# The first sixteen rows of wq, from column 4608 on, sent as transfers of their own from SyncE and GpSimd

## The chip, the cores and the metric

The kernel runs on one core of one Trainium2 chip. The metric is the device time of one execution in microseconds (us); three executions of the kernel before gave 675.35, 675.76 and 675.85, a median of 675.76.

## The reference, cut to what matters

One decode step for two sequences: an attention over a cache of 4096 positions with 16 heads of 256, and a small feed-forward, mixed by a gate. All numbers are float32.

```
g = sigmoid((x * gate_w).sum(-1))                    # x: 2 x 1 x 448
q = x @ wq                                           # wq: 448 x 4096, 16 heads of 256
p = softmax(q . k_cache / 16)                        # 2 x 16 heads x 4096 positions
a = (p . v_cache) @ wo                               # wo: 4096 x 448
b = relu(x @ w1) @ w2                                # 448 x 1792 x 448
out = g * a + (1 - g) * b
```

The two caches hold 32 units (sequence and head), each with 4 MB of keys and 4 MB of values. Every byte of them is used once.

## The kernel before, in words

All operands are laid out on the host so that a load is a plain block: 128 rows, one for each partition, and a contiguous run in each row. `kv` holds the 32 units, each 128 rows of 16,384 numbers (8,192 KB); `wq` is 128 rows of 14,336; `w12` (w1 and w2) 128 rows of 12,544; `wo` 128 rows of 14,336; `xg` (x and gate_w) 128 rows of 12. Three SBUF buffers, `slot0` to `slot2`, take the large loads in turn (L110, L116).

SyncE (SP) issues every large load, in the order in which they are to run (L121 to L144): wq into slot2, the first two units into slot0 and slot1, then in a loop (L126) one unit for each buffer that VectorE has released, and in `late` (L135) w12 in two parts and wo in five, cut at the columns of `CUTS` (L98). ScalarE issues xg (L121). Before each load into a used buffer SP takes the semaphore `free` of that buffer (L63 to L65), which VectorE's last multiplication on that buffer raises (L269). So SP has always asked for one whole unit beyond the one that is under way.

TensorE first waits for xg, computes the gate, then waits for wq and computes q (L187 to L224). From there each unit goes through three engines: TensorE multiplies query and keys (L242), ScalarE takes the exponential (L254), VectorE takes the maximum (L261) and multiplies by the values (L265). Behind the loop TensorE does the feed-forward from w12, and the projection with wo in steps `k` (L364): each of the five parts of wo has a semaphore of its own, and TensorE waits for it at the step where that part begins. The last part holds one step of 32. The result is copied once (L389) and stored (L394).

GpSimd (POOL) only makes an identity matrix (L148, L149), which VectorE reads at L155.

Of the kernel before, what the change touches and what calls it, by code (L numbers as in the profile page):

```python
# [6 lines left out]
AX = mybir.AxisListType  # L7

P, HP = 128, 64
G = 4  # L10
R = P // G
SLOTS = 3
NB = 2
ENGINES = ("tensor", "vector", "scalar", "gpsimd", "sync")
# [48 lines left out]
def take(e, sem, n=1):  # L63
    e.wait_ge(sem, n)
    e.sem_inc(sem, -n)  # L65


def gated_mix_decode(nc, xg, kv, wq, w12, wo, out):
    U, _, LEN = kv.shape
    KC, B = xg.shape[1], xg.shape[2] - 1  # L70
    KF = KC - 1
    D = KF * P + HP
    H = U // B
# [3 lines left out]
    S = LEN // (2 * T)  # L77
    SG = S // G
    NF = w12.shape[1] // 2 // D
    DG = D // G  # L80
    FG = NF * P // G
    RB = R // B
    HB = H // NB
    UB = U // NB
    HH = HB // G
    CW = 512
# [4 lines left out]
    def sbuf(name, *shape):  # L91
        return nc.alloc_sbuf_tensor(name, [*shape], F32).ap()

    def bank(name, n=CW):
# [2 lines left out]
    NO = NB * HH * J  # L97
    CUTS = (0, NO - 18, NO - 8, NO - 4, NO - 1, NO)  # L98
    TAIL = 8
    names = [*ENGINES, "xg", "w2", *(f"wo{k}" for k in CUTS[1:]), "query", "score", "top", "prob", "room",  # L100
             *(f"land{s}" for s in range(SLOTS)), *(f"free{s}" for s in range(SLOTS)), "out"]
    sem = {n: nc.alloc_semaphore(n) for n in names}
    land = [sem[f"land{s}"] for s in range(SLOTS)]
    free = [sem[f"free{s}"] for s in range(SLOTS)]
    pr = Program(nc)
    pe, dve, act, pool, sp = ENGINES
# [3 lines left out]
    slot = [sbuf(f"slot{s}", P, LEN) for s in range(SLOTS)]  # L110
# [5 lines left out]
    def load(s, src, signal, lo=0, hi=None):  # L116
        hi = src.shape[1] if hi is None else hi
        return lambda e: e.dma_start(slot[s][:, lo:hi], src[:, lo:hi]).then_inc(signal, 16)  # L118

    xg_sb = sbuf("xg_sb", P, KC, B + 1)  # L120
    pr.raw(act, lambda e: e.dma_start(xg_sb, xg).then_inc(sem["xg"], 16))  # L121
    pr.raw(sp, load(2, wq, land[2]))
    for u in range(2):
        pr.raw(sp, load(u, kv[u], land[u]))

# [9 lines left out]
    def late(e):  # L135
# [4 lines left out]
        for lo, hi in zip(CUTS, CUTS[1:]):  # L140
            load(0, wo, sem[f"wo{hi}"], lo * D, hi * D)(e)
        take(e, free[1])

    pr.raw(sp, late)  # L144

    ident = sbuf("ident", P, P)

# [1 line left out]
    have_ident = pr.op(pool, lambda e: e.affine_select(  # L149
        out=ident, in_=ident, compare_op=ALU.not_equal, fill=1.0, base=0, pattern=[[-1, P]], channel_multiplier=1),  # L150
        have_ident)


    sel = sbuf("sel", P, R)
    t = pr.op(dve, lambda e: e.tensor_reduce(sel, ident.rearrange("p (g r) -> p r g", g=G), axis=AX.X, op=ALU.add),  # L155
              have_ident)
    fsum = sbuf("fsum", P, B)
    t = pr.op(dve, lambda e: e.tensor_reduce(fsum, sel.rearrange("p (b r) -> p b r", b=B), axis=AX.X, op=ALU.add), t)
# [3 lines left out]


    xr = sbuf("xr", P, KC, G, B, RB)
    pr.raw(dve, lambda e: e.wait_ge(sem["xg"], 16))
    for g in range(G):
        pr.op(dve, lambda e, g=g: e.tensor_copy(xr[:, :, g], xg_sb[:, :, :B, None].to_broadcast([P, KC, B, RB])))  # L167
    xu = sbuf("xu", P, KC, UB // B, B)
# [5 lines left out]
    def flat(a):  # L174
        return a.rearrange("p b r -> p (b r)")

    def mm(out, lhs, rhs, start, stop, *after):
        return pr.op(pe, lambda e: e.matmul(out, lhs, rhs, start=start, stop=stop), *after)  # L178
# [4 lines left out]
    def activate(out, src, fn, *after, **kw):  # L183
        return pr.op(act, lambda e: e.activation(out, src, fn, **kw), *after)  # L184


    pr.raw(pe, lambda e: e.wait_ge(sem["xg"], 16))  # L187
    for c in range(KC):
        r = rows_of(c)
        t = mm(pw[0][:, :1], xr[r, c].rearrange("p g b r -> p (g b r)"), xg_sb[r, c, B:], c == 0, c == KC - 1, have_x)  # L190
# [4 lines left out]
    for c in range(KC):  # L195
        r = rows_of(c)
        t = mm(pw[1][:UB, :1], xu[r, c].rearrange("p u b -> p (u b)"), xg_sb[r, c, B:], c == 0, c == KC - 1)
# [3 lines left out]

    qt = sbuf("qt", P, T, U)
    W = 2 * KF * DH
    WQ = wq.shape[1] // NB
    wide = sbuf("wide", P, CW)
    pr.raw(pe, lambda e: take(e, land[2], 16))
    busy = [(), ()]
    for i in range(NB):
        w = slot[2][:, i * WQ:(i + 1) * WQ]
        for c in range(KC):  # L210
            for g in range(G):
                r = rows_of(c, g // 2)
                at = g * W + c * CW if c < KF else G * W + g % 2 * CW
                lhs, rhs = flat(xr[r, c, g]), w[r, at:at + CW]
                last = mm(pw[2 + i][g * R:(g + 1) * R, :], lhs, rhs, c == 0, c == KC - 1)
        t = activate(wide, pw[2 + i], AF.Copy, last, *busy[1], scale=SCALE)
# [4 lines left out]
        for s in range(2):  # L221
            dst = qt.rearrange("p t (i g s b) -> p i s t g b", i=NB, g=G, s=2)[:, i, s]
            src = pt[:, ::RB].rearrange("p (s t g b) -> p s t g b", s=2, t=T, g=G)[:, s]
# [7 lines left out]
    prob = sbuf("prob", P, SG)  # L231
    query = [sbuf(f"query{s}", P, T) for s in range(SLOTS)]
# [94 lines left out]
    w1, w2 = slot[2][:, :NF * D], slot[2][:, NF * D:]  # L327
    pr.raw(pe, lambda e: take(e, land[2], 16))
    half = NF * D // 2
    for c in range(KC):  # L330
        for g in range(G):
            j, i = divmod(g, 2)
            at = i * half + (j * KF + c if c < KF else 2 * KF) * FG
            r = rows_of(c, j)
            t = mm(ph[g * R:(g + 1) * R, :FG], flat(xr[r, c, g]), w1[r, at:at + FG], c == 0, c == KC - 1)
    t = activate(hs, ph[:, :FG], AF.Relu, t, have_omg, *busy[1], scale=omg)
# [23 lines left out]
    n = NO - TAIL  # L360
# [3 lines left out]
    def project(lo, hi):  # L364
        for k in range(lo, hi):
            if k in CUTS:
                pr.raw(pe, lambda e, s=sem[f"wo{CUTS[CUTS.index(k) + 1]}"]: e.wait_ge(s, 16))
            if k < n:
                g = k % G
                t = mm(acc[g * R:(g + 1) * R, :], lhs(k), w[:, k * D:(k + 1) * D], False, k >= n - G,  # L370
                       have_ot[k // (HH * J)])
            else:
                for g in range(G):
                    t = mm(z[g * R:(g + 1) * R, :DG], lhs(k), w[:, k * D + g * DG:k * D + (g + 1) * DG], k == n,
                           k == NO - 1)
        return t

    at = 0
# [3 lines left out]
    t = project(at, n)  # L382
    t = pr.op(dve, lambda e: e.tensor_copy(a_sb, acc), t)  # L383
# [3 lines left out]
    t = project(CUTS[-3], NO)  # L387
    res = sbuf("res", P, DG)
    t = pr.op(dve, lambda e: e.tensor_copy(res, z[:, :DG]), t)  # L389
# [66 lines left out]
```

## Time and profile before

| what | us |
|---|---|
| three executions, median (range) | 675.76 (675.35 to 675.85) |
| the profiled execution | 675.61 |
| its span, first to last instruction | 674.3 |
| outside the span | 1.3 |
| DMA queue of SP, share of 16 engines' span | 99.3% |
| bytes moved | 289.66 MB |
| VectorE busy | 341.5 |
| TensorE busy | 215.7 |
| ScalarE busy | 59.8 |
| first load (wq), issue to landing | 19.6 |

An engine of the core and a DMA engine are different things. The core has five engines that compute or issue (PE, VectorE as DVE, ScalarE as ACT, GpSimd as POOL, SyncE as SP); the 16 DMA engines move the bytes of the transfers that SP, ACT and POOL issue. A group of instructions is named by its line, its engine and its operation, then what it writes and reads; in brackets stands the idle time before it and what ended that. The DMA share of a window is the mean busy share of the 16 DMA engines in it; a packet is booked whole where it starts, so that short windows with long packets can show more than 1.

### The profile page before, as it was taken

Reading aid. Unit: us, or ns where it says so; the run is one execution under the profiler, and the core shown is the slowest. Engines: PE = TensorE matmul, PEld = TensorE weight load, DVE = VectorE, ACT = ScalarE, POOL = GpSimd, SP = SyncE. Lnnn points to the kernel's source line nnn. Section 1 sums busy time; section 2 is a strip of 40 time slices with the busy share of each in tenths; the row PEclk is TensorE's granted clock in tenths of the full one; section 3 lists DMA queues with packets and bytes.
Section 4 is the critical chain, followed back from the end, with each engine's and each line's share of the span. In section 5 each row is a group of like instructions: output and inputs, shape, how many; then the busy total and the mean of one; then the engine's idle time right before and its main releaser. Section 6 shows DMA issues by size and latency. Waiting matters only on the chain. (4 is left out here: it accounts for less than half of the span.)

```text
span 674.3 us, 4158 instructions
## 1 busy us (share of the span) xinstructions
PE 215.7 (32%) x1323; PEld 65.4 (10%) x1323; DVE 341.5 (51%) x571; ACT 59.8 (9%) x121; POOL 0.7 (0%) x6
## 2 busy tenths in 40 slices
PE   0633221333332123333321233333222333331376
PEld 0210000001001000100100010010000001000022
DVE  0015566544556664454656545455665544556662
ACT  0020001001000100100010010000001001000010
POOL 0000000000000000000000000000000000000000
PEclk9975567767655676776567677665567667656789
DMA  9999999999999999999999999999999999999997
GB/s 381 428 435 436 436 435 435 435 435 435 435 435 435 435 435 435 435 432 435 435 435 435 435 435 435 435 435 435 432 435 435 435 435 435 435 435 435 393 439 309
DMA packets 6052, 289.66 MB, mean 430 GB/s; under 512 B 928, under 2 KB 1056, under 8 KB 1312
## 3 DMA queue, kind: packets, MB, share of 16 engines
q1 hardware_dynamic: 5904, 289.60, 99.3%
q8 instruction: 3, 0.05, 0.0%
q10 hardware_dynamic: 144, 0.01, 0.0%
q14 instruction: 1, 0.01, 0.0%
HBM read 289.54 MB, written 0.06 MB: 429 GB/s over the span
## 5 line engine op out<-in xcount | busy, mean ns | idle before, releaser
L265 DVE SCALAR_TENSOR_TENSOR slot<-slot,prob 128x1024 f32<-128x1024 f32 x256 | 295.9, 1220 | 65.3 <-DVEq L65 65.3
L242 PE MATMUL ps<-slot,query 128*32 128x512 f32 x1024 | 184.0, 880 | 410.8 <-PEq L65 410.7
L261 DVE TENSOR_REDUCE nm<-ps 128x1024 f32 (+1 forms) x32 | 39.2, 1224 | 229.7 <-DVEq L65 229.7
L242 PEld LDWEIGHTS ps<-slot,query 128*32 128x32 f32 x1024 | 53.2, 154 | 539.9 <-issue 539.8
L254 ACT ACTIVATE prob<-ps,nm 128x1024 f32<-128x1024 f32 x32 | 35.7, 1114 | 384.6 <-ACTq L65 384.5
L254 ACT ACT_TABLE_LOAD x10 | 12.8, 1283 | 163.3 <-ACTq L65 163.3
L265 DVE DVE_READ_ACCUMULATOR slot<-slot,prob (+1 forms) x256 | 21.0, 82 | 0.0
L178 PE MATMUL pw<-slot,xr 128*32 128x512 f32 (+3 forms) x96 | 12.4, 646 | 1.4 <-PEq L65 1.4
L167 DVE COPY xr<-xg_sb 128x128 f32<-128x128 f32 x4 | 0.6, 221 | 18.2 <-DMA xg_sb<-in_xg 18.2
L178 PE MATMUL pw<-xg_sb,xr 128*128 128x1 f32 (+1 forms) x8 | 1.9, 352 | 21.4 <-DVE xu L169 21.4
L178 PE MATMUL acc<-slot,ot 128*32 128x448 f32 x48 | 5.9, 545 | 4.1 <-DMA slot<-in_wo 4.1
L249 ACT ACTIVATE query<-qt 128x2 f32 (+1 forms) x32 | 6.2, 193 | 0.0
L254 ACT ACTIVATION_READ_ACCUMULATOR prob<-ps,nm (+1 forms) x32 | 6.2, 193 | 0.0
L178 PE MATMUL acc<-slot,hr 128*32 128x448 f32 x28 | 4.9, 808 | 2.2 <-DMA slot<-in_w 2.2
L181 PE MATMUL pw<-ident,nm 128*16 128x128 f32 x2 | 0.7, 330 | 12.6 <-DVEq L315 12.6
L178 PEld LDWEIGHTS pw<-xg_sb,xr 128*128 128x128 f32 (+1 forms) x8 | 1.8, 320 | 21.4 <-DMA xg_sb<-in_xg 21.4
L178 PEld LDWEIGHTS pw<-slot,xr 128*32 128x32 f32 (+1 forms) x96 | 2.9, 119 | 9.4 <-issue 9.4
L383 DVE COPY wide<-acc 128x448 f32<-128x448 f32 x1 | 0.6, 625 | 4.9 <-PE pw L178 4.9
L181 PE MATMUL pw<-ident,wide 128*128 128x128 f32 x11 | 1.9, 288 | 2.4 <-ACT wide L184 2.4
L309 DVE COPY ot<-pw 128x256 f32<-128x256 f32 x4 | 1.5, 420 | 1.4 <-PE pw L178 1.4
L178 PE MATMUL pw<-slot,ot 128*32 128x112 f32 x64 | 2.2, 261 | 0.0
L301 DVE TENSOR_TENSOR os<-ov,pw 128x128 f32<-128x128 f32 x2 | 0.6, 288 | 3.0 <-PE pw L178 3.0
(42 smaller groups left out, 20.6 us busy)
## 6 DMA issues: line engine op xcount, KB each, us to landing
slot<-in_wq SPq DMA_DIRECT2D x1, 7168.0 KB, 19.6
slot<-in_w SPq DMA_DIRECT2D x2, 3136.0 KB, 30.5
slot<-in_wo SPq DMA_DIRECT2D x1, 3136.0 KB, 20.7
slot<-in_wo SPq DMA_DIRECT2D x1, 2240.0 KB, 25.9
slot<-in_wo SPq DMA_DIRECT2D x1, 896.0 KB, 27.4
slot<-in_wo SPq DMA_DIRECT2D x1, 672.0 KB, 28.5
slot<-in_kv SPq DMA_DIRECT2D x32, 38.5
slot<-in_wo SPq DMA_DIRECT2D x1, 224.0 KB, 28.6
```

The source lines that it names most:

```text
L167: pr.op(dve, lambda e, g=g: e.tensor_copy(xr[:, :, g], xg_sb[:, :, :B, None].to_broadcast([P, KC, B, RB])))
L178: return pr.op(pe, lambda e: e.matmul(out, lhs, rhs, start=start, stop=stop), *after)
L181: return pr.op(pe, lambda e: e.transpose(out, src, ident), *after)
L242: m = e.matmul(ps[g * R:(g + 1) * R, c * CW:(c + 1) * CW], query[s][:, t:t + 1].to_broadcast([P, R]), slot[s][:, lo:lo + CW], start=(t == ...
L249: e.activation(query[s], qt[:, :, bass.ds(u, 1)].rearrange("p t o -> p (t o)"), AF.Copy).then_inc(sem["query"], 1)
L254: e.activation(prob, ps, AF.Exp, bias=nm[:, bass.ds(u, 1)], accum_out=ls[:, bass.ds(u, 1)]).then_inc(sem["prob"], 1)
L261: e.tensor_reduce(nm[:, bass.ds(u, 1)], ps, axis=AX.X, op=ALU.max, negate=True).then_inc(sem["top"], 1)
L265: m = e.scalar_tensor_tensor(v, v, 1.0, prob, op0=ALU.mult, op1=ALU.mult, accum_out=ov[:, bass.ds(u, 1), j])
L301: t = pr.op(dve, lambda e: e.tensor_tensor(os, ov[:, us], wp[:, :UB, None].to_broadcast([P, UB, J]), op=ALU.mult), t)
L309: t = pr.op(dve, lambda e, hh=hh: e.tensor_copy(ot[:, i, hh], po[:, hh * B * J:(hh + 1) * B * J].rearrange("p (b j o) -> p j b o", j=J, o= ...
L383: t = pr.op(dve, lambda e: e.tensor_copy(a_sb, acc), t)
```

## The change

Before, wq came with one transfer of 128 rows, and xg with one of 128 rows. After it:

- wq is cut at column 4608. The first part, all 128 rows of columns 0 to 4607, is still one transfer (`wqm`, 18,432 bytes a row).
- Of the other 9728 columns (38,912 bytes a row), rows 16 to 127 are one transfer of 112 rows (`wqn`).
- Rows 0 to 7 of these columns are issued by GpSimd, in two transfers of four rows (`fan1`, `fan3`). Each row is given as two halves that don't touch in the source (64 numbers of padding, `GAP`).
- Rows 8 to 10 are one transfer of SP with three rows (`wqa`), and rows 11 to 15 are five transfers of SP with one row each (`wqd`).
- The first sixteen rows of xg come from GpSimd too, nine and seven (`fan0`, `fan2`), in turn with fan1 and fan3; ScalarE's xg transfer keeps 112 rows.
- VectorE and TensorE wait for more semaphores at the same places (`x_there`, `wq_there`). GpSimd waits for its four transfers behind the identity matrix and drains, and SP's `late` waits for that.

The bytes are the same, and so is every instruction that computes.

```
FAN, GAP = (9, 4, 7, 4), 64
...
+    def fan_out(e):
+        at = [0, 0]
+        for k, (n, src) in enumerate(zip(FAN, fan)):
+            dst = (x_rows, w_rows)[k % 2]
+            lo = at[k % 2]
+            at[k % 2] += n
+            width = dst.shape[1] // 2
+            e.dma_start(dst[lo:lo + n].rearrange("p (t c) -> p t c", t=2),
+                        src[:, :2 * (width + GAP)].rearrange("p (t c) -> p t c", t=2)[:, :, :width]).then_inc(
+                            sem[f"fan{k}"], 16)
...
+    def first(e):
+        load(2, wqm, land[2])(e)
+        e.dma_start(w_rows[WF:WF + NA], wqa).then_inc(sem["wq"], 16)
+        lo = WF + NA
+        for k in range(ND):
+            e.dma_start(w_rows[lo + k:lo + k + 1], wqd[k:k + 1]).then_inc(sem["wq"], 16)
+        e.dma_start(w_rows[lo + ND:], wqn).then_inc(sem["wq"], 16)
+
+    pr.raw(pool, fan_out)
+    pr.raw(act, lambda e: e.dma_start(x_rows[XF:], xg).then_inc(sem["xg"], 16))
+    pr.raw(sp, first)
...
+    def wq_there(e):
+        take(e, land[2], 16)
+        for k in range(1, len(FAN), 2):
+            e.wait_ge(sem[f"fan{k}"], 16)
+        e.wait_ge(sem["wq"], 16 * (ND + 2))
...
-    pr.raw(act, lambda e: e.dma_start(xg_sb, xg).then_inc(sem["xg"], 16))
-    pr.raw(sp, load(2, wq, land[2]))
...
+    pr.raw(pool, fan_done)
+    pr.raw(sp, late, pr.op(pool, lambda e: e.drain()))
...
+    WL = wq.shape[1] * 19 // 28
+    XF, WF = sum(FAN[::2]), sum(FAN[1::2])
+    wqm, rest = wq[:, :-WL], wq[:, -WL:]
+    fan = [gapped((xg, rest)[k % 2][sum(FAN[k % 2:k:2]):][:n]) for k, n in enumerate(FAN)]
+    arrays = {**{f"fan{k}": a for k, a in enumerate(fan)}, "xg": xg[XF:], "wqm": wqm, "wqn": rest[16:],
+              "wqa": rest[WF:WF + 3], "wqd": rest[WF + 3:16], "kv": kv, "w12": w12, "wo": wo}
```

The start of SP's queue before; a row is a line, an operation, what it writes and reads, its rows and columns, and the semaphores that it waits for:

```order
L60 UNCONDITIONAL_BRANCH [waits barrier_Pool_Activation_PE_DVE_SP_release]
L118 DMA slot2<-in_wq 128x14336
L118 DMA slot0<-in_kv 128x16384
L118 DMA slot1<-in_kv 128x16384
L46 UNCONDITIONAL_BRANCH
L131 ISA [waits free2]
L131 DMA slot2<-in_kv 128x16384
```

The same place after the change:

```order
L61 UNCONDITIONAL_BRANCH [waits barrier_Pool_Activation_PE_DVE_SP_release]
L119 DMA slot2<-in_wqm 128x4608
L152 DMA slot2<-in_wqa 3x9728
L155 DMA slot2<-in_wqd 1x9728 x5
L156 DMA slot2<-in_wqn 112x9728
L119 DMA slot0<-in_kv 128x16384
L119 DMA slot1<-in_kv 128x16384
```

The one load of wq has become eight: 128 rows, three, five times one, and 112. The two units of the cache stand seven instructions later.

GpSimd's queue after the change, from its first instruction behind the barrier; before, it began with the MEMSET of `ident`:

```order
L140 DMA xg_sb<-in_fan0 9x2x6
L140 DMA slot2<-in_fan1 4x2x4864
L140 DMA xg_sb<-in_fan2 7x2x6
L140 DMA slot2<-in_fan3 4x2x4864
L197 MEMSET ident 128x128
L198 ISA [waits gpsimd]
L198 AFFINE_SELECT ident<-ident 128x128
L452 UNCONDITIONAL_BRANCH [waits fan2,fan3,fan1,fan0]
```

Four transfers stand ahead of the identity matrix now, and GpSimd waits for all of them at its end.

More of the change, by code (lines that the diff above doesn't have):

```diff
@@ L9 @@
 P, HP = 128, 64
+FAN, GAP = (9, 4, 7, 4), 64
 G = 4
@@ L65, in take, with gated_mix_decode @@
     e.sem_inc(sem, -n)
-def gated_mix_decode(nc, xg, kv, wq, w12, wo, out):
+def gated_mix_decode(nc, KC, B, fan, xg, wqm, wqn, wqa, wqd, kv, w12, wo, out):
     U, _, LEN = kv.shape
-    KC, B = xg.shape[1], xg.shape[2] - 1
     KF = KC - 1
@@ L99, in gated_mix_decode @@
     TAIL = 8
-    names = [*ENGINES, "xg", "w2", *(f"wo{k}" for k in CUTS[1:]), "query", "score", "top", "prob", "room",
-             *(f"land{s}" for s in range(SLOTS)), *(f"free{s}" for s in range(SLOTS)), "out"]
+    names = [*ENGINES, "xg", "wq", *(f"fan{k}" for k in range(len(FAN))), "w2", *(f"wo{k}" for k in CUTS[1:]), "query",
+             "score", "top", "prob", "room", *(f"land{s}" for s in range(SLOTS)), *(f"free{s}" for s in range(SLOTS)),
+             "out"]
     sem = {n: nc.alloc_semaphore(n) for n in names}
@@ L120, in gated_mix_decode, with fan_done, x_there @@
     xg_sb = sbuf("xg_sb", P, KC, B + 1)
-    pr.raw(act, lambda e: e.dma_start(xg_sb, xg).then_inc(sem["xg"], 16))
-    pr.raw(sp, load(2, wq, land[2]))
+    WM, WL = wqm.shape[1], wqn.shape[1]
+    NA, ND = wqa.shape[0], wqd.shape[0]
+    x_rows = xg_sb.rearrange("p c b -> p (c b)")
+    w_rows = slot[2][:, WM:WM + WL]
+    XF = P - xg.shape[0]
+    WF = FAN[1] + FAN[3]
+    def fan_out(e):
[8 more added lines that the diff above has]
+                            sem[f"fan{k}"], 16)
+        assert at == [XF, WF]
+    def fan_done(e):
+        for k in range(len(FAN)):
+            e.wait_ge(sem[f"fan{k}"], 16)
+        e.dma_reset(range(sem["fan0"].num, sem["fan0"].num + len(FAN)))
+    def first(e):
[8 more added lines that the diff above has]
+    pr.raw(sp, first)
+    def x_there(e):
+        for k in range(0, len(FAN), 2):
+            e.wait_ge(sem[f"fan{k}"], 16)
+        e.wait_ge(sem["xg"], 16)
+    def wq_there(e):
+        take(e, land[2], 16)
+        for k in range(1, len(FAN), 2):
+            e.wait_ge(sem[f"fan{k}"], 16)
+        e.wait_ge(sem["wq"], 16 * (ND + 2))
     for u in range(2):
@@ L142, in late @@
         take(e, free[1])
-    pr.raw(sp, late)
     ident = sbuf("ident", P, P)
@@ L164, in gated_mix_decode @@
     xr = sbuf("xr", P, KC, G, B, RB)
-    pr.raw(dve, lambda e: e.wait_ge(sem["xg"], 16))
+    pr.raw(dve, x_there)
     for g in range(G):
@@ L184, in activate @@
         return pr.op(act, lambda e: e.activation(out, src, fn, **kw), *after)
-    pr.raw(pe, lambda e: e.wait_ge(sem["xg"], 16))
+    pr.raw(pe, x_there)
     for c in range(KC):
@@ L203, in gated_mix_decode @@
     W = 2 * KF * DH
-    WQ = wq.shape[1] // NB
+    WQ = (WM + WL) // NB
     wide = sbuf("wide", P, CW)
-    pr.raw(pe, lambda e: take(e, land[2], 16))
+    pr.raw(pe, wq_there)
     busy = [(), ()]
@@ L445, with gapped @@
     w12 = np.concatenate([w1, w2], 1)
-    arrays = {"xg": xg, "kv": kv, "wq": wq, "w12": w12, "wo": wo}
+    def gapped(a):
+        a = np.pad(a.reshape(len(a), 2, -1), [(0, 0), (0, 0), (0, GAP)])
+        return np.pad(a.reshape(len(a), -1), [(0, 0), (0, GAP)])
+    xg = xg.reshape(P, -1)
+    WL = wq.shape[1] * 19 // 28
[4 more added lines that the diff above has]
+              "wqa": rest[WF:WF + 3], "wqd": rest[WF + 3:16], "kv": kv, "w12": w12, "wo": wo}
     arrays = {n: np.ascontiguousarray(a) for n, a in arrays.items()}
@@ L451 @@
     out = nc.dram_tensor("out_0", (P, D // G), F32, kind="ExternalOutput").ap()
-    gated_mix_decode(nc, *args, out)
+    gated_mix_decode(nc, KF + 1, B, args[:len(FAN)], *args[len(FAN):], out)
     r = run_bass_kernel_spmd(nc, [{f"in_{n}": a for n, a in arrays.items()}], core_ids=[0])
```

## The prediction

> **What bounds the kernel now.** I read the page's busy times and slices first, then the DMA queues, the sizes and landing times of the loads, the windows of the steady part, and last the chain of waits with the windows and the timeline of the final microseconds.
>
> From the page, span and slices (each digit a tenth of a fortieth of the span):
>
> ```profile
> span 674.3 us, 4158 instructions
> ...
> DMA  9999999999999999999999999999999999999997
> DMA packets 6052, 289.66 MB, mean 430 GB/s; under 512 B 928, under 2 KB 1056, under 8 KB 1312
> ...
> q1 hardware_dynamic: 5904, 289.60, 99.3%
> ...
> q10 hardware_dynamic: 144, 0.01, 0.0%
> ```
>
> From the windows, the long middle part (the last two columns are the DMA share and GB/s):
>
> ```profile
> 60.00:620.00 560.00, 166.72 (x928) 48.74 (x920) 303.69 (x492) 49.20 (x96) 0.00 (x0) 0.63 1.00 434
> ```
>
> The 16 DMA engines are full from the start to the end: a share of 1.00 for 560 us at 434 GB/s, while VectorE, the busiest of the others, works 304 of these 560 us. So one DMA engine moves 434 / 16 = 27.1 GB/s all the time, and the time is bytes over rate plus what lies at the two ends. Nothing on a computing engine can change that.
>
> The packet counts say how a transfer is cut. Queue q1 carries SP's 41 transfers (wq, 32 units, two of w12, five of wo, and the store), all of 128 rows: 41 x 128 = 5248 packets, and the other 656 are 41 x 16. Queue q10 carries xg alone: 144 = 128 + 16. So **one row is one packet**, and each of these transfers adds one small packet per DMA engine. A packet is on one engine, so every engine has 8 rows of each transfer.
>
> Do the engines ever run dry? From the DMA issues, with the median us from issue to landing, and from SP's waits:
>
> ```profile
> slot<-in_kv SPq DMA_DIRECT2D x32, 38.5
> ```
>
> ```profile
> SPq L65 <- SPq L65: 634.7, 34, 33.4
> ```
>
> A unit of 8,192 KB (8.39 MB) takes 8.39 MB / 434 GB/s = 19.3 us; it lands 38.5 us after its issue. So 19.2 us of work lie queued ahead of it, and SP waits for buffers, not DMA engines for SP. An engine that falls behind by less than some 19 us never makes the other fifteen wait, and nothing gives it back what it lost: **a row more on one DMA engine at the start is a row more at the end.**
>
> Now the end, from the chain of waits and the timeline of TensorE:
>
> ```profile
> 641.77 25.89 DMA slot<-in_wo
> 667.66 0.04 issue
> 667.70 2.27 PE acc L178 x19
> 669.98 2.41 PE pw L178 x71
> 672.41 0.28 DVE res L389
> ```
>
> ```profile
> 667.70 2.45 PE L178 MATMUL acc<-slot,ot 128*32 128x448 f32 x20 [1.85 <-DMA slot<-in_wo]
> 669.69 1.23 PE L178 MATMUL pw<-slot,ot 128*32 128x112 f32 x32
> ...
> 671.29 0.97 PE L178 MATMUL pw<-slot,ot 128*32 128x112 f32 x32
> ```
>
> TensorE idles 1.85 us until the second part of wo has landed at 667.66, and the 4.6 us behind that are work with later parts landing in between. A landing needs all 16 engines, so this time is set by the slowest of them. How far apart are they? The windows of the last transfers, in order of time:
>
> ```profile
> 669.00:669.40 0.40, 0.40 (x10) 0.12 (x2) 0.00 (x0) 0.00 (x0) 0.00 (x0) 1.00 0.87 345
> 669.40:669.80 0.40, 0.40 (x8) 0.11 (x6) 0.00 (x0) 0.00 (x0) 0.00 (x0) 1.00 0.95 372
> 669.80:670.20 0.40, 0.40 (x19) 0.40 (x20) 0.00 (x0) 0.00 (x0) 0.00 (x0) 1.00 0.33 130
> 670.20:670.60 0.40, 0.40 (x24) 0.40 (x16) 0.38 (x1) 0.00 (x0) 0.00 (x0) 1.00 0.24 99
> 670.60:671.00 0.40, 0.40 (x14) 0.17 (x10) 0.25 (x1) 0.00 (x0) 0.00 (x0) 1.00 0.21 81
> 671.00:671.50 0.50, 0.50 (x16) 0.27 (x20) 0.00 (x0) 0.00 (x0) 0.00 (x0) 1.00 0.10 36
> 671.50:672.00 0.50, 0.50 (x30) 0.50 (x24) 0.00 (x0) 0.00 (x0) 0.00 (x0) 1.00 0.00 0
> ```
>
> Until 669.8 the share is near 1, then it falls to 0.33, 0.24 and 0.21, and a tenth is left until 671.5: about twelve engines end together near 669.8, and some four straggle for up to 1.7 us. The idle engine time from 669.0 to 671.5, shared over 16, is 0.4 x (0.13 + 0.05 + 0.67 + 0.76 + 0.79) + 0.5 x 0.90 = 1.4 us. That is **all that a perfect distribution of rows could win**, 0.21% of 675.76.
>
> **The change part by part.**
>
> *The price of a row.* A row of the cut part is 38,912 bytes: 38,912 / 27.1 GB/s = 1.44 us of one DMA engine. The first part, wqm, leaves 8 rows on each engine, wqn has 112 / 16 = 7 rows for each. So each engine is one row short of what it had, and the 16 rows that go alone decide who gets how many. An engine that gets none is 1.44 us ahead of one that gets one; that is the size of the stragglers' delay.
>
> *The eight rows of GpSimd and the three of wqa.* Given to eight and three different engines, they just restore these to 8 rows. No transfer of before has fewer than 16 rows, and none comes from GpSimd, so the trace doesn't show where they land. Bounds: 0 (eleven different engines), and 1.44 us more where one of them falls on an engine that has too much already. I take 0.
>
> *The five rows of wqd* are the disputed part. Each is a transfer of its own with one row. By the packet counts a row is one packet, so none of them can be spread; each lies wholly on one engine. Which? The five instructions are alike in shape, queue and semaphore, and only the address differs. If the shape settles the engine, as nothing in the counts speaks for a state that moves from transfer to transfer, all five go to the same one. The ends are 0 rows too many (five engines that have 7) and 5 rows too many on one. I take five, since that is what five like instructions give.
> [...]
>
> So one engine has 7 + 1 + 5 = 13 rows where it had 8: 5 x 1.44 = **+7.18 us** of data. It also has 13 more packets of rows or so and about ten small ones; from the 1.00 share with eight packets per unit these are hundredths of a us, and I add 0.1.
>
> *What of it reaches the end.* The delay stays (above), less that engine's lead over the last one at the end. The windows give the lead: 1.4 us for the mean engine, 671.4 - 669.8 = 1.6 for one of the twelve, 0 for the last straggler. I take 1.6: 7.18 + 0.1 - 1.6 = **+5.7 us**; bounds +5.4 for the earliest engine (669.6 in place of 669.8, rounded) and +7.3 for the last straggler. The work of TensorE behind each landing moves along unchanged, since all five parts of wo cross the same late engine one after the other.
>
> *SP's queue.* Seven more issues stand ahead of the units:
>
> ```profile
> 0.75 0.39 SPq L118 DMA_DIRECT2D slot<-in_wq  x1
> 1.19 0.90 SPq L118 DMA_DIRECT2D slot<-in_kv  x2
> 35.85 565.00 SPq L131 DMA_DIRECT2D slot<-in_kv  x30
> ```
>
> At 0.39 to 0.45 us each, wqn is issued near 0.75 + 7 x 0.43 = 3.8 us, not yet late: wqm alone (2.36 MB) keeps the engines busy for 5.4 us from their start near 2 us. The first unit goes out near 4.2 us in place of 1.2 and is wanted near 20. Cost 0; without the cover of wqm it would be up to 3 us.
>
> *GpSimd's queue.* Four issues go ahead of the identity matrix. Their cost isn't in the trace; the nearest rows are SP's 0.4 us each, so 1.6 us at least. VectorE's three small sums read the identity, and stand ahead of its wait for xg:
>
> ```profile
> 1.50 0.37 DVE L155 TENSOR_REDUCE sel<-ident 128x32 f32<-128x128 f32 x1 [1.50 <-POOL ident L149]
> ...
> 20.55 0.63 DVE L167 COPY xr<-xg_sb 128x128 f32<-128x128 f32 x4 [18.25 <-DMA xg_sb<-in_xg]
> ...
> 21.43 1.92 PE L178 MATMUL pw<-xg_sb,xr 128*128 128x1 f32 x8 [21.43 <-DVE xu L169]
> ...
> 23.66 5.25 PE L178 MATMUL pw<-slot,xr 128*32 128x512 f32 x32
> ```
>
> VectorE then idles 18.25 us: even 10 us of issue would be covered. SP's `late` waits for GpSimd near 620 us, when its transfers of the first 10 us are long done: 0.
>
> *xg comes sooner.* Its packets took turns with wq's long rows and landed with the last of them. In turn with rows of 18,432 bytes (0.68 us each) seven of them are through after about 5 us. The gate is done early and q starts as soon as wq is there, a gain of about 3 us at 23.66. It is worth nothing at the end: q is first needed when the first unit lands near 40 us. Against that wq lands 7.2 us later on the late engine, near 27.5, and SP's next issue moves from 35.85 to about 40; the DMA engines have work in their queues until 2 + 17 + 2 x 19.3 = 58 us. So this cover holds as well, with 18 us to spare.
>
> The sum: the profiled execution had 675.61 with a span of 674.3; a span of 680.0 and 1.3 around it give 681.3. Its time is 0.15 under the median, so the median goes to 675.76 + 5.7, or about **681.5 us** (+0.8%).
>
> **The rivals.**
>
> *The rows even the engines out* (faster, the other side). The five rows go to different engines or are cut into pieces, and the engines left with less are the four or five stragglers. Speaking for it: a row of 1.44 us is close to the 1.7 us by which they come late, and about eleven of the 16 engines get a row. Against it: the packet counts, one row one packet, and five alike instructions. If each engine got its even share, 5 / 16 = 0.31 row or 0.45 us, and the stragglers lost 1.44 - 0.45 = 0.99 us, the end would come 1.7 - max(0.45 + 0.34, 0.71) = 0.9 us sooner, with 0.34 as an estimate for the spread of the twelve, taken from the 0.4 us window in which they end: 674.9. The point that decides is whether two of the five rows share an engine: from there on nothing is won.
> [...] SP's rows in the order show 1x9728, unsplit.
>
> *Fewer rows pile up.* A choice of engine that moves, or goes by partition, puts two to four of the rows on one engine, or a GpSimd row on top: 2 x 1.44 - 1.6 = +1.3 to 4 x 1.44 - 1.6 = +4.2 us, 677.0 to 680.0; a sixth row on top of the five gives +7.1, 682.9. Nothing in the trace shows such a state.
>
> *The late engine is hidden.* If the buffers gave slack at the end, the delay would be swallowed: 675.8. Against it stands the idle 1.85 us of TensorE ahead of 667.70: it waits for a landing already.
>
> **How the numbers follow.** Five rows on one engine: 0.78, with 681.1 to 683.1 as its own range (+5.4 to +7.3). Fewer piled up: 0.06. Evened out: 0.11. Hidden: 0.05. The range of 680.0 to 683.5 takes the first case with a sixth row or a straggler at its upper end, and the four-row case at its lower one. It leaves out the cases near 675 and two or three rows, about 2 in 10. A measurement of this kernel can tell about 0.2% (1.35 us) from no change. Slower by more than that: 0.84 (the first case and the piled-up ones). Within it: 0.14 (evened out, as its 0.9 us is under 1.35, and hidden). Faster: 0.02, since even a perfect distribution wins just 1.4 us.
>
> **What would show it.** Right: the rate of the middle part stays 434 GB/s; in the windows of the last transfers the share falls to near 1/16 (0.06) and stays there for some 5 us, where before it had 0.2 for one; wq lands near 27 us; TensorE's idle time ahead of the second part of wo grows from 1.85 to over 7 us; SP's issues of units stay 19.3 us apart but come later by 7. Wrong: a steep fall from 1 to 0 within a us means that the rows were spread, and a tail of 1.5 to 4 us that fewer piled up. If the first microseconds show a share under 1 between wqm and wqn, SP's issues weren't covered, and all engines lose that.

## The result, and the profile after

The changed kernel takes **702.09 us** (median of 6 runs, 701.23 to 702.83) against 675.73 for the kernel before in the same job: a ratio of 1.0391, 95% interval 1.0378 to 1.0404, or +26.4 us. The direction was forecast; the size was not, +5.7 with a range that ended at 683.5. The profiled execution took 702.83, with a span of 701.5.

The page of the changed kernel, the lines that answer to those of before:

```profile
span 701.5 us, 4176 instructions
...
DMA  9999999999999999999999999999999999999992
GB/s 239 242 390 433 433 439 430 441 437 426 430 441 437 426 430 448 433 422 430 448 437 422 433 441 437 426 441 437 430 426 445 437 426 430 448 433 422 418 372 98
DMA packets 6340, 289.66 MB, mean 413 GB/s; under 512 B 1080, under 2 KB 1208, under 8 KB 1464
...
q1 hardware_dynamic: 6048, 289.29, 97.5%
q0 software_dynamic: 160, 0.31, 0.3%
```

The DMA digits are 9 to the last slice as before, and still the first two slices, 35 us, move 239 and 242 GB/s in place of 381 and 428. The windows below have a share of 0.96 to 1.04 at 182 to 392 GB/s and of 1.00 at 434: a DMA engine counts as busy while a packet is under way, however slowly. So the share alone no longer says that the engines work at their rate; the GB/s beside it does. The packets agree with one row, one packet, and with no spreading: q1 has 41 + 7 = 48 transfers with 5368 rows, and the other 680 packets are 42 x 16 + 3 + 5 x 1, so the transfer of three rows has three small packets and each single row has one.

The windows of the first 58 us and of the long middle part (last columns: DMA share, GB/s):

```profile
8.00:18.00 10.00, 0.00 (x0) 0.00 (x0) 0.00 (x0) 0.00 (x0) 0.00 (x0) 1.00 0.96 182
18.00:28.00 10.00, 2.31 (x16) 2.21 (x16) 0.89 (x6) 0.33 (x2) 0.00 (x0) 1.00 1.04 249
28.00:38.00 10.00, 0.00 (x0) 0.00 (x0) 0.00 (x0) 0.00 (x0) 0.00 (x0) 1.00 1.00 284
38.00:48.00 10.00, 0.00 (x0) 0.00 (x0) 0.00 (x0) 0.00 (x0) 0.00 (x0) 1.00 1.02 392
48.00:58.00 10.00, 8.00 (x52) 2.25 (x56) 0.00 (x0) 0.86 (x3) 0.00 (x0) 1.00 0.95 413
58.00:640.00 582.00, 177.70 (x984) 53.64 (x976) 307.25 (x497) 52.83 (x104) 0.00 (x0) 0.63 1.00 434
```

From 8 us, when the rows of columns 4608 and up begin, to 48 us the engines run at 182 to 392 GB/s; from 58 on everything is at 434 again. And the windows of the end:

```profile
684.00:686.00 2.00, 2.00 (x20) 0.52 (x12) 0.95 (x2) 0.00 (x0) 0.00 (x0) 0.84 0.98 410
686.00:688.00 2.00, 0.67 (x4) 0.10 (x2) 0.79 (x5) 0.26 (x1) 0.00 (x0) 1.00 0.64 248
688.00:690.00 2.00, 0.57 (x8) 0.16 (x8) 0.00 (x0) 0.00 (x0) 0.00 (x0) 1.00 0.12 49
690.00:692.00 2.00, 2.00 (x32) 0.89 (x28) 0.37 (x2) 0.00 (x0) 0.00 (x0) 1.00 0.10 35
692.00:694.00 2.00, 1.15 (x12) 0.12 (x2) 0.67 (x2) 0.00 (x0) 0.00 (x0) 1.00 0.06 27
694.00:696.00 2.00, 1.22 (x16) 0.48 (x18) 0.00 (x0) 0.00 (x0) 0.00 (x0) 1.00 0.05 22
696.00:698.00 2.00, 2.00 (x47) 1.02 (x39) 0.62 (x1) 0.00 (x0) 0.00 (x0) 1.00 0.07 29
```

At 686 to 688 most engines end; then the share lies at 0.05 to 0.12, one or two of 16 engines, for ten us. That is the tail of one overloaded engine, twice as long as forecast. So there are two losses: most engines end near 687 in place of 670, and one ends some 10 us behind them.

Two rows of TensorE's timeline show the start:

```profile
21.72 1.92 PE L230 MATMUL pw<-xg_sb,xr 128*128 128x1 f32 x8 [21.72 <-DVE xu L221]
...
49.21 5.71 PE L230 MATMUL pw<-slot,xr 128*32 128x512 f32 x32 [25.18 <-DMA slot<-in_wqn]
```

q starts at 49.21 us instead of 23.66, waiting for the rows of wq.

The profile's records of packets don't name the DMA engine, but the rows of the late one can be followed back from the last row of wq: each begins within 40 ns of the end of the one before it, and no other record fits more closely. Start and duration in ns, first a row of wqm (18,432 bytes), then thirteen rows of 38,912 bytes:

```
wqm:     7686 2086
13 rows: 9811 4207   14047 2938   16999 2588   19596 2889   22487 2825   25314 1740
         27057 2721  29774 3165   32936 2952   35884 3221   39102 2815   41913 3044   44953 3044
```

Thirteen rows is what was forecast for this engine. They took 38.2 us, 2.94 us each in place of 1.44. The last row on any other engine ended at 33.5 us; this engine's ended at 48.0.

### The profile page after: what moved, and what is told of

It reads as the page before. It is cut to its first block, busy times and chain, and to the rows that moved or that the text cites. A ratio compares the mean times of both kernels' runs of the same rounds, so it can differ in the third digit from the quotient of the medians.

```text
span 701.5 us, 4176 instructions
## 1 busy us (share of the span) xinstructions
PE 217.8 (31%) x1323; PEld 67.8 (10%) x1323; DVE 341.5 (49%) x571; ACT 59.8 (9%) x121; POOL 3.1 (0%) x10
## 5 line engine op out<-in xcount | busy, mean ns | idle before, releaser
L294 PEld LDWEIGHTS ps<-slot,query 128*32 128x32 f32 x1024 | 55.7, 155 | 538.3 <-issue 538.2
```

The source lines that it names most:

```text
L294: m = e.matmul(ps[g * R:(g + 1) * R, c * CW:(c + 1) * CW], query[s][:, t:t + 1].to_broadcast([P, R]), slot[s][:, lo:lo + CW], start=(t == ...
```

## The experiments

Four theories for the 26.4 us. **Place:** a transfer of 128 rows gives each DMA engine eight partitions of its own; with other row counts engines write each other's partitions and slow each other. **Source:** rows of 38,912 bytes are read slowly. **GpSimd:** its transfers slow all. **Pile:** one engine has too many rows, and nothing else is wrong. In the expectations they are A, B, C and D. Times are medians; those of the kernel before in the three jobs were 675.64, 675.60 and 675.62.

### wq in two parts by columns (e1_two_column_parts)

```
-    pr.raw(sp, load(2, wq, land[2]))
...
+    pr.raw(sp, load(2, wqm, land[2]))                                        # 128 rows, columns to 4607
+    pr.raw(sp, lambda e: e.dma_start(w_rows, wqn).then_inc(sem["wq"], 16))   # 128 rows, the other 9728
```

> The kernel before with wq in two transfers of 128 rows, cut at column 4608, so that the second has rows of 38,912 bytes like the changed kernel. Four theories for the 26.4 us. A, place: a transfer of 128 rows gives each DMA engine partitions of its own, any other row count deals rows out in another way, and engines that write the same group of partitions slow each other. B, source: rows of 38,912 bytes are read slowly. C, GpSimd: its transfers slow all. D, pile: one engine has five rows too many, and nothing else is wrong. A, C and D: 675.7, within 0.7. B: the rows take the 3 us each that the changed kernel's first 48 us imply at about half the rate, so +10 us or more, over 685.

Measured: 675.9 us, ratio 1.0001 (0.9990 to 1.0013). Its windows:

```profile
8.00:18.00 10.00, 2.30 (x16) 2.20 (x16) 0.89 (x6) 0.33 (x2) 0.00 (x0) 1.00 1.00 434
18.00:28.00 10.00, 5.73 (x33) 1.27 (x34) 0.00 (x0) 0.60 (x1) 0.00 (x0) 1.00 1.11 479
```

The same rows of 38,912 bytes move at the full 434 GB/s when they come as 128, and each of the 128 packets took 1,439 ns, the price of the forecast. The source theory falls, as far as it rests on the length of a row.

### 16 and 112 rows, from SyncE alone (e2_rows_16_and_112)

```
+    for lo, hi in ((0, 16), (16, P)):
+        pr.raw(sp, lambda e, lo=lo, hi=hi: e.dma_start(w_rows[lo:hi], wqn[lo:hi]).then_inc(sem["wq"], 16))
```

> As the run of two column parts, but the second part goes as 16 rows and 112 rows, both from SyncE; no GpSimd transfer, and each engine has 8 rows again, one and seven. A: slow, since neither transfer has 128 rows: wq lands 12 us or more later than the 19.6 us of before, and the end moves by +10 to +18 us with no engine far behind the others, 686 to 694. B: the same if rows of 38,912 bytes are slow, but then the run of two column parts is slow as well. C and D: 675.7, as there is no transfer of GpSimd and no pile. [...]

Measured: 688.51 us, ratio 1.0194 (1.0164 to 1.0223), +12.9. The windows of the start, and of the end:

```profile
8.00:18.00 10.00, 2.30 (x16) 2.20 (x16) 0.89 (x6) 0.33 (x2) 0.00 (x0) 1.00 1.03 183
18.00:28.00 10.00, 0.00 (x0) 0.00 (x0) 0.00 (x0) 0.00 (x0) 0.00 (x0) 1.00 1.00 249
```

```profile
680.00:682.00 2.00, 1.80 (x20) 0.56 (x20) 0.00 (x0) 0.00 (x0) 0.00 (x0) 1.00 0.97 401
682.00:684.00 2.00, 2.00 (x48) 1.22 (x42) 0.62 (x1) 0.00 (x0) 0.00 (x0) 1.00 0.29 116
684.00:686.00 2.00, 1.02 (x36) 0.73 (x32) 0.27 (x1) 0.00 (x0) 0.00 (x0) 1.00 0.01 4
```

Without GpSimd, and with eight rows for each engine if each transfer is dealt out evenly (q1 has 6064 packets, 16 small ones for each of the two), the start has the 182 and 249 GB/s of the changed kernel nearly to the digit (183 and 249). There is no tail of one engine. About half of the loss is here, as the place theory forecast. The run doesn't tell the 16 rows, all of them into partitions 0 to 15, from the 112 beside them; what each of the two transfers costs is not shown.

### The five single rows in one transfer (e3_five_rows_in_one)

```
-        for k in range(ND):
-            e.dma_start(w_rows[lo + k:lo + k + 1], wqd[k:k + 1]).then_inc(sem["wq"], 16)
+        e.dma_start(w_rows[lo:lo + ND], wqd).then_inc(sem["wq"], 16)
```

> The changed kernel with its five single-row transfers put into one transfer of five rows; all else stays. If the five single rows lay on one engine, and five rows in one transfer go to five, the late engine loses four rows. A: the engines meet as before, so the common delay stays and the four rows at some 3 us each go: 702.1 - 12 = 690, with no single engine 10 us behind at the end. D: all of the delay goes, 676 to 677. If the single rows lay on five engines already: 702, no change.

Measured: 691.10 us, ratio 1.0232 (1.0202 to 1.0262): 11.0 less than the changed kernel. The windows of its end:

```profile
682.00:684.00 2.00, 1.99 (x24) 0.44 (x18) 0.59 (x2) 0.00 (x0) 0.00 (x0) 1.00 0.97 398
684.00:686.00 2.00, 2.00 (x42) 1.01 (x38) 0.29 (x1) 0.00 (x0) 0.00 (x0) 1.00 0.53 212
686.00:688.00 2.00, 1.76 (x56) 1.03 (x46) 0.33 (x1) 0.00 (x0) 0.00 (x0) 1.00 0.05 21
```

The long tail is gone. So the five single rows did lie on one engine, and taking four of them away saved 11.0 / 4 = 2.8 us each, not 1.44.

### wq as two halves of 64 rows (e4_two_halves_of_64)

```
-    pr.raw(sp, load(2, wq, land[2]))
+    pr.raw(sp, lambda e: e.dma_start(slot[2][:HP, :wq.shape[1]], wq[:HP]).then_inc(land[2], 16))
+    pr.raw(sp, lambda e: e.dma_start(slot[2][HP:, :wq.shape[1]], wq[HP:]).then_inc(sem["wq"], 16))
```

> The kernel before with wq as two transfers of 64 whole rows (partitions 0 to 63, then 64 to 127) in place of one of 128; rows, bytes, source and count of packets stay, and each engine has four rows of each. A: 16 engines write the partitions that 8 engines write in a transfer of 128 rows, so each half goes at half the rate: wq's 7.34 MB takes 34 us in place of 17, landing near 37, and the end moves by +17 us to 692.6. B, C and D: 675.7 (57,344-byte rows, no GpSimd, no pile).

Measured: 694.32 us, ratio 1.0280 (1.0250 to 1.0309), +18.7. Its windows:

```profile
8.00:18.00 10.00, 0.00 (x0) 0.00 (x0) 0.00 (x0) 0.00 (x0) 0.00 (x0) 1.00 0.89 184
18.00:28.00 10.00, 0.00 (x0) 0.00 (x0) 0.00 (x0) 0.00 (x0) 0.00 (x0) 1.00 0.90 189
```

Nothing is new here but the row count: whole rows, one source, SyncE alone, and on q1 the 16 small packets of one transfer more (5920 for 5904). Half the partitions at a time gave less than half the rate, 184 to 189 in place of 217. That it is not just half, and +18.7 where +17 was expected, stays open.

### The halves with another order in the source (e8_halves_rows_alternate)

```
-                                                           wq[:HP]     wq[HP:]
+                                                           wq[0::2]    wq[1::2]     # wq stored to match
```

> The run of two halves of 64 rows, with wq stored in another order: the rows of the two halves alternate in the source, so that each engine reads rows 114,688 bytes apart in place of 57,344, while the partitions written stay. A: the partitions written set the rate, 694.3 within 1 us. If the places read set it: another time by several us, up or down.

Measured: 693.97 us, ratio 1.0271 (1.0251 to 1.0292), as without it (694.32). This other order in the source changes nothing, which leaves the partitions written.

### 16 and 112 rows with half the bytes (e7_rows_16_and_112_half)

```
-"wqm": wq[:, :4608], "wqn": wq[:, 4608:]
+"wqm": wq[:, :9472], "wqn": wq[:, 9472:]
```

> The run of 16 and 112 rows with the cut of wq at column 9472, so that these transfers carry half the bytes (rows of 19,456 bytes). A: the cost goes with the bytes in such transfers, half of the 12.9 us: 682.1. If it went with the count of transfers or of rows: 688.5 as before.

Measured: 682.14 us, ratio 1.0096 (1.0076 to 1.0116), +6.5, half of 12.9. The cost of these two transfers went with their bytes.

### GpSimd's transfers alone (e6_gpsimd_alone)

```
+    pr.raw(pool, fan_out)        # 9, 4, 7 and 4 rows, as in the change, into unused columns of slot2
+    pr.raw(pool, fan_done)
+    gathered = pr.op(pool, lambda e: e.drain())
```

> The kernel before, and GpSimd's four transfers with the changed kernel's shapes (9, 4, 7 and 4 rows in two pieces each, the wide ones 2 x 4,096 bytes) into the unused columns of slot2, waited for and not used; SyncE's late waits for GpSimd's drain as in the changed kernel. Theory C, that GpSimd's transfers slow the others: over 677, and the slices of the first 48 us under 400 GB/s. A and D: 65 KB more, 0.3 us on eight engines, 675.7 to 676.1.

Measured: 676.66 us, ratio 1.0014 (1.0005 to 1.0024), +1.1, a little over what was expected without the GpSimd theory, and far from 26, with rows of 8,192 bytes where the changed kernel has 38,912. The page's slices stay full:

```profile
GB/s 383 430 435 436 432 431 435 435 435 435 435 435 435 435 435 435 435 435 435 435 435 431 435 435 435 431 435 435 435 435 431 431 435 435 435 435 435 404 430 322
```

Here the wide rows go into partitions 9 to 12 and 20 to 23, not into 0 to 7 as in the changed kernel. If the four into 20 to 23 all hold up one engine, as the single rows of e10 below do, their 32,768 bytes are 1.2 us at 27.1 GB/s, an estimate; wq lands 1.2 us later (20.8 for 19.6). That fits, but was not tried apart. The ten times lie between 675.84 and 677.29, and this page is of the execution of 675.84; so it doesn't show where the 1.1 us went.

### 24 single rows more (e5_24_single_rows_more)

```
...
+    def singles(e):
+        for p in range(SINGLES):                                  # 24, behind wq's 128 rows
+            e.dma_start(spare[p:p + 1], wq[p:p + 1, :spare.shape[1]]).then_inc(sem["wq"], 16)
```

> The kernel before, and 24 more transfers of SyncE behind wq, each of one row of 8,192 bytes from wq's first columns into the unused columns of slot2, partitions 0 to 23; they are waited for and not used. 196,608 bytes, as much as the five single rows of the changed kernel within 1%, while wq stays at 128 rows. If single rows all go to one engine: 7.25 us of data there at 27.1 GB/s and 0.5 for the packets, less the 1.6 us lead of a common engine, +6.1 us: 681.8, and a tail of the DMA share near 0.06 for some 5 us. If each goes to another engine or is spread: 1.5 rows or 0.45 us for each, 676.1. If single rows are slow in themselves, at the 3 us that a row of 38,912 bytes took in the changed kernel, +13 or more.

Measured: 687.65 us, ratio 1.0178 (1.0157 to 1.0198), +12.05 where the bytes alone gave +6.1. The windows of its end show one engine, as expected, for longer:

```profile
672.00:674.00 2.00, 0.00 (x0) 0.00 (x0) 0.64 (x4) 0.22 (x1) 0.00 (x0) 1.00 0.37 145
674.00:676.00 2.00, 1.91 (x18) 0.73 (x22) 0.29 (x1) 0.00 (x0) 0.00 (x0) 1.00 0.09 35
676.00:678.00 2.00, 1.81 (x24) 0.43 (x16) 0.76 (x2) 0.00 (x0) 0.00 (x0) 1.00 0.06 27
678.00:680.00 2.00, 0.60 (x8) 0.29 (x12) 0.00 (x0) 0.00 (x0) 0.00 (x0) 1.00 0.06 23
680.00:682.00 2.00, 2.00 (x34) 0.78 (x30) 0.08 (x1) 0.00 (x0) 0.00 (x0) 1.00 0.06 25
```

So the pile is on one engine even with wq left alone, and a single row can cost twice its bytes: the first six took 309 ns each, the others 393 to 701. The forecast of the size was wrong here too.

### Single rows into an engine's own partitions, and into another's (e9, e10)

```
+    ROWS = (0, 1, 2, 3, 32, 33, 34, 35)      # e9_16_singles_own_rows
+    ROWS = (4, 5, 6, 7, 36, 37, 38, 39)      # e10_16_singles_other_rows
...
+        for k in range(2):
+            for p in ROWS:
+                e.dma_start(spare[k][p:p + 1], wq[p:p + 1, k * 2048:(k + 1) * 2048]).then_inc(sem["wq"], 16)
```

> The kernel before with 16 more single-row transfers of 8,192 bytes behind wq (8 into the unused columns of slot2, 8 into a buffer of their own, waited for and not used), all into partitions 0 to 3 and 32 to 35. In the run of 24 single rows the first six took 309 ns and the later ones 394 to 701 ns, one behind the other on one engine. Place: these eight partitions are the ones that the first engine writes in a transfer of 128 rows, so no other engine is met and each row takes 0.31 us: 5.0 us, less the 1.6 us lead, +3.4: 679.1. Time alone (single rows get slow once the other engines have moved on to the next load, wherever they write): the same as the run into other partitions, about 684.

> As the run into partitions 0 to 3 and 32 to 35, but into 4 to 7 and 36 to 39, which another engine writes in a transfer of 128 rows; bytes and count are the same. Place: while that engine is at work too, each of the two gets half, so the 16 rows take some 0.62 to 0.70 us each once the next load has begun, about 10 us, less the 1.6 us lead, +8 to +9: 684, and a second engine is late by up to 5 us. Count or bytes alone: the same as the run into its own partitions.

Measured: 678.95 us (ratio 1.0051, 1.0028 to 1.0074) and 683.62 (1.0120, 1.0091 to 1.0149), where 679.1 and 684 were expected. The two kernels differ in nothing but the eight numbers, each of which is the partition written and the row of wq read; e8, where another order of reading changed nothing, speaks against the row read. The profile's records of the sixteen packets (start and duration in ns; the first three and the last two of each):

```
own:     19732 309   20044 309   20356 309  ...  24097 309   24409 309
other's: 19911 309   20223 309   20534 484  ...  27894 616   28513 619
```

In its own partitions the engine needs 309 ns for every row. In another engine's, the first two rows take 309 as well, the third 484, and all others, while rows of the next load are under way, 600 to 640. The owner of these partitions pays too: three rows of that next load (65,536 bytes each) took 3,895, 4,912 and 3,224 ns in e10, starting at 19,585, 23,467 and 28,366, where none took over 2,422 in the first 48 us of e9. At 620 and 4,912 ns the two engines move 13.2 and 13.3 GB/s, together the 26.5 that 309 ns for 8,192 bytes give for one alone. A window near the end shows the same; first of e9, then of e10:

```profile
672.00:674.00 2.00, 2.00 (x28) 0.71 (x24) 0.00 (x0) 0.00 (x0) 0.00 (x0) 0.94 0.06 26
```

```profile
672.00:674.00 2.00, 2.00 (x28) 0.52 (x20) 0.76 (x2) 0.00 (x0) 0.00 (x0) 1.00 0.13 54
```

0.06 is one of 16 engines, 0.13 is two: in e10 a second engine is late.
That each set of eight partitions belongs to one engine in a 128-row load was an assumption of both runs. They agree with it for these two sets, with 309 against 600 to 640 ns; for no other set was it tried.

## Why the prediction was wrong

*The bound and the mechanism at the end* held. The rate of the middle part stayed at 434 GB/s, the start's loss was never given back, and the end moved with the slowest engine.

*All five single rows on one engine*, thirteen rows in all, held: the tail near 0.06 in the changed kernel, its absence in e3, the same tail in e5, and the thirteen packets one behind the other. None of GpSimd's rows (halves of 19,456 bytes) is among the thirteen, so the 0 taken for them held for this engine. The 7 + 1 + 5 of the forecast can be seen too. At the end of each of the first six of the thirteen rows a small packet starts, within 5 ns (the first at 14,022 ns, the sixth at 27,051): by SP's order the row of wqa and the five of wqd. The next one at the end of such a row comes at 47,993, behind seven rows more, those of wqn. Why the row of wqa lies on the engine of the five no run shows, nor which of the 16 it is; in e9 sixteen single rows ran undisturbed, at 309 ns each, in partitions 0 to 3 and 32 to 35.

*The price of a row* is the step that failed. I divided 38,912 bytes by 27.1 GB/s and took 1.44 us wherever the row goes. The thirteen rows took 2.94 us each on average, and e9 and e10 show why: 309 or some 620 ns for the same 8,192 bytes by where they are written. 27.1 GB/s is the rate of an engine in transfers of 128 rows, and by e10 the eight partitions that it has there take no more from two engines together: 13.2 and 13.3 GB/s, 26.5 in all. Every row of before was 128 of 128, so the trace couldn't show this, and I took the rate for the engine's alone.

*"wqn has 7 rows for each", at no cost*, failed by the same step. I counted rows per engine and never asked which partitions those are. In e2 16 and 112 rows ran at 183 GB/s and then 249. In the changed kernel the last row on any engine but the late one ended at 33.5 us, against 21.1 in e1, much like the 12.9 us of e2. The bytes for each group of partitions are the same as before. That several engines wanted one group while others stood empty fits e4 and e10; which partitions each engine got of the 112 rows is not shown.

The sum, done again for the late engine: its thirteen rows took 38.2 us where eight took 8 x 1.44 = 11.5, its last row of wqm took 2.09 us where 0.69 was usual, and its lead was 1.6. That gives 26.7 + 1.4 - 1.6 = 26.5 us, an estimate, against 26.4 measured; the lead is read from windows of 0.4 us, so that the two agree to a tenth is luck. Of this the five rows too many at the forecast price are 7.2 us, and the price is 13 x (2.94 - 1.44) = 19.5.

The runs cut it in another way, from the medians: 12.9 for 16 and 112 rows in place of 128 (e2), 11.0 for four single rows too many on one engine (from e3), and 2.6 left over between e2 and e3 (691.10 - 688.51). The last may be GpSimd's rows, or engines with more than eight rows in e3, which no run shows; it was not taken apart.

*The lead of 1.6 us* held: with it and 0.31 us a row, e9 came out at 678.95 for 679.1.

*SP's and GpSimd's queues* held. SP's rows after:

```profile
1.60 1.71 SPq L155 DMA_DIRECT2D slot<-in_wqd  x5
...
3.36 0.32 SPq L156 DMA_DIRECT2D slot<-in_wqn  x1
3.72 1.00 SPq L119 DMA_DIRECT2D slot<-in_kv  x2
```

wqn was issued at 3.36 (3.8 forecast) and the units from 3.72 (4.2), both ahead of need. The next unit went out at 61.87 us instead of about 40, as q waited for the late rows; the engines still had work, with 413 GB/s from 48 to 58 us and 434 after.

*One sign did not come*: TensorE's wait ahead of the second part of wo was to grow from 1.85 to over 7 us.

```profile
694.78 2.45 PE L230 MATMUL acc<-slot,ot 128*32 128x448 f32 x20 [1.63 <-DMA slot<-in_wo]
```

The late engine held up every load alike, so the units, w12 and all parts of wo come late together: SP's last unit went out at 627.5 us instead of 600.5.

*xg sooner* was wrong without cost: VectorE got x at 20.84, because GpSimd's seven rows of xg landed only 18.1 us after their issue, behind the slow rows. ScalarE's own 112 rows of it landed after 13.0. In e1, with all of xg on ScalarE, it landed after 9.4.

*The rivals:* evening out did not happen. Its premise, that a row can be moved from a late engine to another, looks doubtful by e10, since the owner is slowed while the other writes (up to 4,912 ns for a row of 65,536 bytes, where e9 has none over 2,422); whether it could win anything was not tried. No run beat the kernel before; e1, which keeps 128 rows in both parts, equals it.

## What to carry to other kernels

Price a transfer by where it writes as well as by its bytes (8,192 bytes took 0.31 us in e9 and 0.60 to 0.64 in e10): count, for each of the 16 engines, the rows and the groups of partitions that it meets, and keep 128 rows together where the DMA engines are the bound (434 GB/s in e1, 184 to 189 with 64 in e4). Read the GB/s beside the DMA share, as a share near 1 says nothing about speed (here 1.04 at 249 and 1.00 at 434). Balance of bytes among engines is worth little if it costs them their own partitions: here at most 1.4 us stood against 26.4 lost.

## What the runs showed of the hardware

- A load of 64 rows into half of the partitions ran at 184 to 189 GB/s (e4), under half of 434; two of them, one after the other, cost 18.7 us more than the one load of 128 rows.
- 16 single-row transfers of SyncE ran one after another on one DMA engine, at 0.31 us for 8,192 bytes into partitions 0 to 3 and 32 to 35, and at 0.60 to 0.64 into 4 to 7 and 36 to 39 beside a 128-row load.
- Two DMA engines that wrote into the same eight partitions shared a rate: 13.2 and 13.3 GB/s in e10, where one alone moved 26.5 into its own (8,192 bytes in 309 ns, e9).
- Small rows of another queue, in turn with long rows, landed as late as the long ones: xg after 19.8 us beside rows of 57,344 bytes, after 9.4 beside 18,432 (e1). In e4 and e8 the same xg landed after 1.8 and 1.7 us beside rows of 57,344: there its packets started at 1.7 to 2.2 us, with or ahead of the first rows, and in the kernel before from 4.6 us on.
